# Alibi attention and a SwiGLU block on one core: loads in order of need, masks derived on chip, four tiles ahead of the FFN

## The chip, the core and the metric

One NeuronCore of a Trainium2 chip. The metric is the time of one execution on the device in microseconds (us), lower is better; the median of three runs of the kernel before is 411.18 us (411.11 to 411.30).

## What is computed

q, k and v have 8 batches, 8 heads, 576 positions and 64 columns. Attention looks back over 128 positions with a bias that falls with the distance; its output, 4608 rows of 512 columns, goes through a SwiGLU block of width 1536. Cut to what matters:

```python
scores = scale * np.matmul(q, k.transpose(0, 1, 3, 2))
slopes = 2.0 ** (-8.0 * (np.arange(H) + 1) / H)
mask = (rel >= 0) & (rel < 128)            # rel = query position - key position
scores = np.where(mask, scores - slopes[:, None, None] * np.abs(rel), -1e9)
attn = softmax(scores)
x = np.matmul(attn, v).transpose(0, 2, 1, 3).reshape(B * S, H * D)
g = x @ w_gate
out = (g * sigmoid(g) * (x @ w_val)) @ w_out
```

Inputs and output are float32; on the chip everything that TensorE reads is float16.

## The kernel before

**Tiles and units.** The eight batches are taken as four pairs (s = 0 to 3). A pair has nine tiles of 128 rows: four of the first batch, one made of the last 64 rows of both (two DMAs per tensor), and four of the second batch. Tiles are numbered 0 to 35 over the pairs (`ranks`). A pair also has nine units (queries of 128 rows); unit i needs the tiles up to `need_rank[i]`, which for a pair are 1, 2, 3, 4, 6, 7, 8, 8, 8.

**Attention for a unit** has four steps. The tile's k and q (`kn`, `qn`) are transposed on TensorE into one PSUM tile `pt` (L162, L164) and copied by VectorE to `kT` and `qT` (L165, L166). Scores `ps` (L209) go through ScalarE's exp into `exr` (L223) and are multiplied on VectorE with a mask that holds the bias and the window (L227). With those as weights TensorE takes v, whose 65th column is ones (`va`, L254); VectorE divides by that column (L256, L257) into `x`. TensorE transposes x (`px`, L281), and ScalarE copies it to `xT` (L282).

**Masks.** There are four, all loaded over the queue of SyncE: `reg` for most units, `lo` and `hi` for the units beside the shared tile, `com` for the shared tile itself.

**The FFN** runs over nine blocks of 512 rows. Block n takes units 4n and so on (block 0: units 0 to 3; block 8: the four shared units). For each of 12 slices m of 128 columns a generator `gate_val` does four matmuls for the gate (`pg`, L295), tanh on ScalarE (L298), a VectorE step `uu` (L300), four matmuls for the value (`pv`, L308) and their product `hT` (L310). A `pg` with its `pv` is called a pair here, each of the two a group. The projection of block n-1 (`po`, L322, 12 matmuls for each of four row tiles) is mixed into block n after m = 1 to 4.

**Order.** Code order is mixed by hand: `att_step` advances attention by one of eight steps per unit, and after each FFN step as many are taken as keep 4.55 units per 36 FFN steps. `ready[n]` says how many units must be finished ahead of block n. A scheduler then fixes each engine's order. Tile i + 8 is loaded in unit i, and the transposes for unit i + 2 are issued in unit i, two units ahead of need. In front of block 0 stand units 0 to 3, with the transposes up to tile 7 and the scores of unit 4.

**Loads.** k, q, v and the three weights are loaded over GpSimd's queue (POOL), which turns float32 into float16. In order: tiles 0 and 1; columns 0 to 128 of the gate and value weights; tiles 2 and 3; columns 128 to 512; tile 4; columns 512 to 1536 of both; tile 5; w_out; tiles 6 and 7; the rest as buffers come free (four of k and q, 14 of v). Each DMA waits, on POOL, for the landing of the eighth before it.

Of the kernel before, what the change touches and what calls it, by code (L numbers as in the profile page):

```python
# [10 lines left out]
FP16 = mybir.dt.float16  # L11
# [6 lines left out]
QK_BY_DMA = False  # L18
X_BY_DMA = False
# [7 lines left out]
def slot_c(h):  # L27
    return 4 * (h % 2) + h // 2


def make_masks(H):

    slopes = [2.0 ** (-8.0 * (h + 1) / H) for h in range(H)]
    j = np.arange(P)[:, None]
    i = np.arange(P)[None, :]

    def weight(h, u, ok):
        return np.where(ok & (u >= 0) & (u < WIN), np.exp(-slopes[h] * np.maximum(u, 0)), 0.0)

    reg = np.zeros((P, H, 256), np.float32)  # L40
    lo = np.zeros((P, H, 256), np.float32)
    hi = np.zeros((P, H, 256), np.float32)
    com = np.zeros((P, H, 128), np.float32)
    every = np.ones((P, P), bool)
    for h in range(H):
        s = slot(h)
        diag = weight(h, i - j, every)
        for m in (reg, lo, hi):
            m[:, s, 0:128] = diag
        reg[:, s, 128:256] = weight(h, i - j + 128, every)  # L50
        lo[:, s, 128:256] = weight(h, i - j + 128, (i < 64) & every)
        hi[:, s, 128:256] = weight(h, i - 64 - j + 128, (i >= 64) & every)
        com[:, slot_c(h), :] = weight(h, i - j, (i < 64) == (j < 64))
    return [m.astype(np.float16) for m in (reg, lo, hi, com)]
# [3 lines left out]
def kernel(  # L58
# [16 lines left out]
    NSUP = B // 2  # L75
    scale = 1.0 / np.sqrt(D)

    reg, lo, hi, com = make_masks(H)
# [5 lines left out]
    mask = {}  # L84
    for name, m in (("reg", reg), ("lo", lo), ("hi", hi), ("com", com)):
        m_d = nc.inline_tensor(m, name="mask_" + name)
        mask[name] = (consts.tile(list(m.shape), FP16, name="m_" + name), m_d)

    def load_mask(name):
        t, d = mask[name]  # L90
        nc.sync.dma_start(t, d.ap())

    load_mask("reg")
# [9 lines left out]
    vpool = ctx.enter_context(tc.tile_pool(name="vp", bufs=14))  # L103
# [4 lines left out]
    hpool = ctx.enter_context(tc.tile_pool(name="hp", bufs=2))  # L108
# [4 lines left out]

    units = []
    for s in range(NSUP):
        for p in range(9):
            units.append(dict(s=s, p=p))  # L120
    ranks = [(s, r) for s in range(NSUP) for r in range(9)]

# [6 lines left out]
    def pieces(s, c):  # L129
        if c == 4:  # L130
            return [(0, 64, 2 * s, 512), (64, 128, 2 * s + 1, 512)]
        b, t = (2 * s, c) if c < 4 else (2 * s + 1, c - 5)
        return [(0, 128, b, t * P)]

    def load(rank):
        s, c = ranks[rank]
        tq = nat.tile([P, H, D], FP16, name="qn", tag="qn")
        tk = nat.tile([P, H, D], FP16, name="kn", tag="kn")
        tv = vpool.tile([P, H, D + 1], FP16, name="va", tag="va")
        nc.gpsimd.memset(tv[:, :, D:D + 1], 1.0)  # L140
        for t_, src in ((tk, k), (tq, q), (tv, v)):
            for p0, p1, b, r0 in pieces(s, c):
                nc.gpsimd.dma_start(  # L143
                    t_[p0:p1, :, 0:D],
                    src[b, :, r0:r0 + p1 - p0, :].rearrange("h p d -> p h d"))
        natq[rank], natk[rank], va[(s, c)] = tq, tk, tv

    def transposes(rank):
        s, c = ranks[rank]
        if c == 0:  # L150
            qTs[s] = tpool.tile([P, 4, 9 * P], FP16, name="qT", tag="qT")
            kTs[s] = tpool.tile([P, 4, 9 * P], FP16, name="kT", tag="kT")
        cols = slice(c * P, (c + 1) * P)
        tq, tk = natq.pop(rank), natk.pop(rank)
        if QK_BY_DMA:
            for t_, dst in ((tk, kTs[s]), (tq, qTs[s])):
# [3 lines left out]
        pt = ps_a.tile([P, 8, P], FP16, name="pt", tag="a")  # L160
        for j in range(4):
            nc.tensor.transpose(pt[:, j, :], tk[:, 2 * j:2 * j + 2, :], idm)  # L162
        for j in range(4):
            nc.tensor.transpose(pt[:, 4 + j, :], tq[:, 2 * j:2 * j + 2, :], idm)  # L164
        nc.vector.tensor_copy(kTs[s][:, :, cols], pt[:, 0:4, :])  # L165
        nc.vector.tensor_copy(qTs[s][:, :, cols], pt[:, 4:8, :])  # L166
# [3 lines left out]
    def scores(i):  # L170

        s, p = units[i]["s"], units[i]["p"]
# [3 lines left out]
        if p == 8:  # L176
# [9 lines left out]

            def act(par):
                nc.scalar.activation(er[:, 4 * par:4 * par + 4, :], banks[par], AF.Exp, scale=scale)

            def mul():  # L190
                nc.vector.tensor_mul(e, er, mask["com"][0])

            return [[lambda: act(0)], [lambda: act(1), mul], [], []]
# [25 lines left out]
        m = mask["lo" if p == 3 else "hi" if p == 7 else "reg"][0]  # L219
# [14 lines left out]
    def weighted(i):  # L234

        s, p = units[i]["s"], units[i]["p"]
        x = xpool.tile([P, H, D], FP16, name="x", tag="x")
        xs[i] = x
        for half in range(2):
            av = ps_a.tile([P, 4, D + 1], FP32, name="av", tag="a")  # L240
            todo = []
            for j in range(4):
                h = 4 * half + j
                if p == 8:
                    todo.append((j, ex[(s, 3)][:, slot(h), 128:256], va[(s, 3)][:, h, :]))
                    todo.append((j, ex[(s, 7)][:, slot(h), 128:256], va[(s, 8)][:, h, :]))
# [15 lines left out]
    def place(i):  # L262

        s, p = units[i]["s"], units[i]["p"]
        if p == 8:
            return 8, s
# [212 lines left out]
```

## Time and profile before

| | |
|---|---|
| median of three runs | 411.18 us |
| the profiled execution | 410.85 us |
| its span, first to last instruction | 409.1 us |
| TensorE busy | 364.4 us, 89% |
| VectorE busy | 245.9 us, 60% |
| ScalarE busy | 173.8 us, 42% |
| mean granted TensorE clock | 0.997 |
| read from HBM, written | 39.62 MB, 9.44 MB |

TensorE's busy time counts pipelined matmuls and is no measure of how well its array is used; what matters is where it is idle, and who ended that. In the rows of the profile an instruction is named by its line in the kernel, its engine, and what it writes and reads, as `kT<-pt`; PE is TensorE, PEld its weight loads, DVE VectorE, ACT ScalarE, POOL GpSimd, SP SyncE.

### The profile page before, as it was taken

To read this page: it belongs to the slowest core of one execution; us is meant where nothing else is said; L and a number is where in the kernel's file an instruction comes from. 1 tells how busy PE (TensorE), PEld (TensorE's weight loads), DVE (VectorE), ACT (ScalarE), POOL (GpSimd) and SP (SyncE) were. 2 spreads that over 40 slices of the span, in tenths; PEclk is the share of its full clock that TensorE was granted. 3 is DMA by queue.
4 is the path that set the end of the run, shared out by engine and by line. 5 is a ranking of instruction groups with operands and counts; after the bars stand their busy time and mean duration, and the time that the engine had idled before them with its cause. 6 is when DMAs were issued, how large, how long until landed. Compare 5 with 4: busy or idle time off the path is not lost.

```text
span 409.1 us, 6645 instructions
## 1 busy us (share of the span) xinstructions
PE 364.4 (89%) x2592; PEld 181.0 (44%) x2592; DVE 245.9 (60%) x500; ACT 173.8 (42%) x317; POOL 112.0 (27%) x170
## 2 busy tenths in 40 slices
PE   0571289999999999999999999999999999999995
PEld 0240134455545445444454454455544445444442
DVE  0351057876587567675885586758865864572550
ACT  1241055534455455445644555455444543323321
POOL 7974485053424211542260104111000000000000
PEclk9999999999999999999999999999999999999998
DMA  9999999269969652799696527654011000101104
GB/s 221 164 192 193 182 155 95 14 42 80 124 66 66 64 79 38 52 82 116 64 68 63 79 38 48 82 79 29 0 53 51 2 27 26 51 2 51 54 12 91
DMA packets 124304, 30.62 MB, mean 75 GB/s; under 512 B 114544, under 2 KB 119152, under 8 KB 124272
## 3 DMA queue, kind: packets, MB, share of 16 engines
q0 software_dynamic: 118304, 18.88, 62.0%
q1 hardware_dynamic: 5968, 11.31, 8.1%
q8 instruction: 20, 0.33, 0.3%
q14 instruction: 12, 0.10, 0.1%
HBM read 39.62 MB, written 9.44 MB: 120 GB/s over the span
## 4 chain that ended last, share of the span: by engine, by line
PE 73%; DMA 10%; DVE 7%; ACT 5%; issue 2%; POOL 1%; DVEq 0%; POOLq 0%; ACTq 0%
PE po L322 22%; PE pv L308 20%; PE pg L295 20%; DMA kn<-in_k_dram 6%; DMA wv_sb<-in_moe_w_val_dram 4%; ACT exr L223 4%; PE ps L209 3%; PE av L254 3%; PE px L281 3%; DVE uu L300 2%; PE pt L162 1%; PE pt L164 1%; DVE hT L310 1%; DVE exl L227 1%; DVE ex L227 1%
## 5 line engine op out<-in xcount | busy, mean ns | idle before, releaser
L308 PE MATMUL pv<-xT,wv_sb 128*128 128x512 f16 x432 | 112.0, 380 | 1.4 <-DVE uu L300 1.2
L295 PE MATMUL pg<-xT,wg_sb 128*128 128x512 f16 x432 | 112.0, 381 | 0.3
L300 DVE SCALAR_TENSOR_TENSOR uu<-tt,pg 128x512 f16<-128x512 f16 x108 | 73.8, 684 | 61.6 <-ACT tt L298 61.2
L322 PE MATMUL po<-wo_sb,hT 128*128 128x512 f16 x432 | 104.8, 379 | 0.9 <-ACT osb L326 0.7
L298 ACT ACTIVATE tt<-pg 128x512 f16<-128x512 f32 x108 | 65.1, 603 | 79.5 <-PE pg L295 77.6
L223 ACT ACTIVATE exr<-ps 128x512 f16<-128x512 f32 x128 | 67.4, 608 | 39.7 <-PE ps L209 39.7
L310 DVE TENSOR_TENSOR hT<-uu,pv 128x512 f16<-128x512 f16 x108 | 74.0, 685 | 8.3 <-PE ps L209 1.0
L143 POOL DMA_DIRECT2D kn<-in_k_dram x40 | 34.0, 853 | 113.3 <-PE pt L164 101.9
L308 PEld LDWEIGHTS <-wv_sb 128*128 128x128 f16 x432 | 40.8, 98 | 47.4 <-issue 4.4
L322 PEld LDWEIGHTS <-hT 128*128 128x128 f16 x432 | 40.0, 98 | 43.7 <-issue 3.9
L295 PEld LDWEIGHTS <-wg_sb 128*128 128x128 f16 x432 | 39.9, 98 | 43.8 <-issue 3.2
L227 DVE TENSOR_TENSOR ex<-exr,m_reg 128x1024 f16<-128x1024 f16 x48 | 33.1, 689 | 36.2 <-ACT exr L223 36.2
L326 ACT ACTIVATE osb<-po 128x512 f32<-128x512 f32 x36 | 21.6, 600 | 59.0 <-PE po L322 58.9
L282 ACT COPY xT<-px 128x512 f16<-128x512 f16 x36 | 21.0, 584 | 50.9 <-PE px L281 50.8
L162 PE MATMUL pt<-idm,kn 128*128 128x128 f16 x144 | 15.7, 238 | 27.9 <-DMA kn<-in_k_dram 27.0
L143 POOL DMA_DIRECT2D va<-in_v_dram x40 | 33.8, 851 | 7.3 <-POOL va L140 5.0
L143 POOL DMA_DIRECT2D qn<-in_q_dram x40 | 34.1, 854 | 5.1 <-DMA wo_sb<-in_moe_w_out_dram 2.9
L165 DVE COPY kT<-pt 128x512 f16<-128x512 f16 x36 | 15.1, 418 | 31.6 <-PE pt L164 31.4
L257 DVE TENSOR_TENSOR x<-av,rec 128x256 f16<-128x256 f32 x72 | 29.0, 419 | 0.7
L209 PE MATMUL ps<-qT,kT 64*128 64x256 f16 (+1 forms) x288 | 27.2, 282 | 2.3 <-DVE qT L166 2.3
L162 PEld LDWEIGHTS <-kn 128*128 128x128 f16 x144 | 11.1, 105 | 35.4 <-DMA kn<-in_k_dram 29.1
L281 PE MATMUL px<-idm,x 128*128 128x128 f16 x144 | 18.8, 230 | 5.5 <-DVE x L257 5.4
(27 smaller groups left out, 173.5 us busy)
## 6 DMA issues: line engine op xcount, KB each, us to landing
out_dram<-osb SPq DMA_DIRECT2D x32, 256.0 KB, 2.0
kn<-in_k_dram POOLq DMA_DIRECT2D x32, 128.0 KB, 3.7
qn<-in_q_dram POOLq DMA_DIRECT2D x32, 128.0 KB, 5.0
va<-in_v_dram POOLq DMA_DIRECT2D x32, 128.0 KB, 5.3
wo_sb<-in_moe_w_out_dram POOLq DMA_DIRECT2D x2, 768.0 KB, 16.4
wg_sb<-in_moe_w_gate_dram POOLq DMA_DIRECT2D x2, 512.0 KB, 8.7
wv_sb<-in_moe_w_val_dram POOLq DMA_DIRECT2D x2, 512.0 KB, 10.1
out_dram<-osb SPq DMA_DIRECT2D x8, 128.0 KB, 2.3
```

Source lines behind the costliest of these rows:

```text
L143: nc.gpsimd.dma_start(t_[p0:p1, :, 0:D], src[b, :, r0:r0 + p1 - p0, :].rearrange("h p d -> p h d"))
L162: nc.tensor.transpose(pt[:, j, :], tk[:, 2 * j:2 * j + 2, :], idm)
L209: nc.tensor.matmul(two[par][:, j, o:o + w], kT[rows, pair, kcols], qT[rows, pair, cols], start=(j == 0 and n == 0), stop=(j == 1 and n == ...
L223: nc.scalar.activation(er[:, o:o + 2, :], banks[q4][par], AF.Exp, scale=scale)
L227: nc.vector.tensor_mul(e[:, o, :], er[:, o, :], m[:, o, :])
L281: nc.tensor.transpose(pt[:, kb, :], x[:, kb * P:(kb + 1) * P], idm)
L295: nc.tensor.matmul(pg, wg_sb[:, kb, ms], xT[n][:, kb, :], start=(kb == 0), stop=(kb == NKB - 1))
L298: nc.scalar.activation(tt, pg, AF.Tanh, scale=0.5)
L300: nc.vector.scalar_tensor_tensor(out=uu, in0=tt, scalar=1.0, in1=pg, op0=ALU.add, op1=ALU.mult)
L308: nc.tensor.matmul(pv, wv_sb[:, kb, ms], xT[n][:, kb, :], start=(kb == 0), stop=(kb == NKB - 1))
L310: nc.vector.tensor_mul(hT[n][:, m, :], uu, pv)
L322: nc.tensor.matmul(po, hT[n][:, m, j * P:(j + 1) * P], wo_sb[:, m, :], start=(m == 0), stop=(m == NMB - 1))
```

## The change

- **Loads** are ordered anew, and k, q and v of a tile are loaded separately: k and q of tile 0, then q, v and k so that each unit's last need comes last, up to tile 4's k (v of tile 4 later); then columns 0 to 128 and 128 to 512 of the two weights; tile 5 and v of tile 4; columns 512 to 1024; tile 6; columns 1024 to 1536; tiles 7 and 8; w_out.
- **Masks**: only `reg` is loaded. `lo`, `hi` and `com` are put together by memsets and copies on VectorE; `com` takes the heads in the same order as the others, for which the exps of the shared unit write with a stride.
- **v's column of ones** is set once for 14 fixed buffers by VectorE, not by POOL for each tile.
- **Transposes**: q and k have a PSUM tile each, q goes first (but for a pair's first tile), and they are issued with the scores that need them, one unit ahead, not two.
- **FFN**: the scores of unit 4 and the transposes for them follow unit 3's end in the code. The first eight FFN steps of block 0 have no attention between them, the other 16 have two attention steps each, and later blocks 5.2 units per 36 steps.
- **hT** has a buffer for each m (18 of them) instead of one for each block (two).

The core of the diff:

```diff
-    load_mask("reg")
+    def make_lo():
+
+        nc.vector.memset(lo[:, :, 192:256], 0.0)
+        nc.vector.tensor_copy(lo[:, :, 0:192], reg[:, :, 0:192])
+
+    def make_hi():
+
+        nc.vector.memset(hi[:, :, 128:192], 0.0)
+        nc.vector.tensor_copy(hi[:, :, 0:128], reg[:, :, 0:128])
+        nc.vector.tensor_copy(hi[:, :, 192:256], reg[:, :, 128:192])
+
+    def make_com():
+
+        nc.vector.memset(com, 0.0)
+        nc.vector.tensor_copy(com[0:64, :, 0:64], reg[0:64, :, 0:64])
+        nc.vector.tensor_copy(com[64:128, :, 64:128], reg[64:128, :, 64:128])
...
+    def transposed(name, rank):
+
+        s, c = divmod(rank, 9)
+        t_, dst = (natk.pop(rank), kTs[s]) if name == "k" else (natq.pop(rank), qTs[s])
+        pt = ps_a.tile([P, 4, P], FP16, name="pt", tag="a")
+        for j in range(4):
+            nc.tensor.transpose(pt[:, j, :], t_[:, 2 * j:2 * j + 2, :], idm)
+        nc.vector.tensor_copy(dst[:, :, c * P:(c + 1) * P], pt)
...
+        for name in ("kq" if c == 0 else "qk"):
+            transposed(name, rank)
...
-            if i < last:
+            if i < last and i != FIRST - 1:
                 transposes_to(need_rank[i + 1])
                 after = scores(i + 1)
-            for n in range(4):
-                for f in after[n]:
+            if i == 1:
+                make_lo()
+            if i == 5:
+                make_hi()
+                make_com()
+            for fs in after:
+                for f in fs:
                     f()
-                if n == 2 and i + 2 <= last:
-                    transposes_to(need_rank[i + 2])
                 yield i
             weighted(i)
             yield i
-            loads_to(i + 8)
+            if i >= FIRST:
+                loads_to(i + 7)
...
+            if i == FIRST - 1:
+
+                transposes_to(need_rank[i + 1])
+                for fs in scores(i + 1):
+                    for f in fs:
+                        f()
+                    yield i + 1
...
-    loads_to(1)
-    load_w(wg2, wg_sb, 0, 128)
-    load_w(wv2, wv_sb, 0, 128)
-    loads_to(3)
...
+    load_qk(0, "kq")
+    for r in range(4):
+        load_qk(r + 1, "q")
+        load_v(r)
+        load_qk(r + 1, "k")
+    load_w(0, 128)
+    load_w(128, 512)
+    load(5)
+    load_v(4)
+    load_w(512, 1024)
+    load(6)
+    load_w(1024, 1536)
+    load(7)
+    load(8)
+    loaded = 9
...
+    for _ in ffn():
         step += 1
-        target = base + step * (4.55 * 8) / per_block
-        while att_done < target and att_step():
-            att_done += 1
+        if step < 24:
+            blk, target = 0, base + 2 * max(0, step - 8)
+        else:
+            blk = min(NBLK - 1, 1 + (step - 24) // 36)
+            target = base + 32 + (step - 24) * RATE * 8 / 36
```

What this does to the engines' order, at three places. First POOL, which issues the loads. Before, from the third slice of the gate weight on (`kn_134` is tile 4, `kn_149` tile 5, `kn_158` tile 6):

```order
L143 DMA kn_134<-in_k_dram 64x8x64 x2
...
L344 DMA wg_sb_65<-in_moe_w_gate_dram 128x4x512
L344 DMA wv_sb_66<-in_moe_w_val_dram 128x4x512
...
L143 DMA kn_149<-in_k_dram 128x8x64
L143 DMA qn_148<-in_q_dram 128x8x64
L143 DMA va_150<-in_v_dram 128x8x64
L404 DMA wo_sb_67<-in_moe_w_out_dram 128x6x512 x2
L140 MEMSET va_159 128x8
L143 DMA kn_158<-in_k_dram 128x8x64
```

The two rows of 512 columns stand there twice. Now, on POOL from the first such slice's predecessor on (`kn_142` is tile 5, `kn_151` tile 6, `kn_158` now tile 7):

```order
L407 DMA wg_sb_65<-in_moe_w_gate_dram 128x4x384
L407 DMA wv_sb_66<-in_moe_w_val_dram 128x4x384
L149 DMA kn_142<-in_k_dram 128x8x64
L149 DMA qn_144<-in_q_dram 128x8x64
L143 DMA va2_102<-in_v_dram 128x8x64
...
L407 DMA wg_sb_65<-in_moe_w_gate_dram 128x4x512
L407 DMA wv_sb_66<-in_moe_w_val_dram 128x4x512
L149 DMA kn_151<-in_k_dram 128x8x64
L149 DMA qn_153<-in_q_dram 128x8x64
...
L149 DMA kn_158<-in_k_dram 128x8x64
```

Tile 5 has moved ahead of four slices of 512 columns, tile 6 ahead of two of them and of w_out, and w_out behind tile 8.

Second, VectorE ahead of the first FFN step `uu`. Before, after unit 3's masks `exl` (`pt_377` is tile 5, `pt_388` tile 6, `pt_457` tile 7, `ex_452` unit 4; the first `uu` comes seven rows below):

```order
L227 TENSOR_TENSOR exl_372<-exr_371,m_lo_61 128x1024 x2
L165 COPY kT_174<-pt_377 128x4x128
L166 COPY qT_173<-pt_377 128x4x128
L165 COPY kT_174<-pt_388 128x4x128
L166 COPY qT_173<-pt_388 128x4x128
...
L257 TENSOR_TENSOR x_401<-av_402,rec_411 128x256
...
L227 TENSOR_TENSOR ex_452<-exr_451,m_reg_60 128x1024
L165 COPY kT_174<-pt_457 128x4x128
```

Now, after unit 3's x (`pt_505` and `pt_511` are q and k of tile 5):

```order
L269 TENSOR_TENSOR x_400<-av_413,rec_422 128x256
L163 COPY qT_170<-pt_505 128x4x128
L163 COPY kT_171<-pt_511 128x4x128
L307 SCALAR_TENSOR_TENSOR uu_439<-tt_437,pg_432 128x512
L314 TENSOR_TENSOR hT_431<-uu_439,pv_441 128x512
```

Of tiles 5, 6 and 7 and unit 4's scores only tile 5 still stands ahead of the FFN.

Third, VectorE further on in block 0, from the fifth pair on (`uu_503`; `pt_517`, `pt_523` are tile 6, `pt_565`, `pt_571` tile 7, `pt_668` tile 8):

```order
L163 COPY qT_170<-pt_517 128x4x128
L307 SCALAR_TENSOR_TENSOR uu_503<-tt_501,pg_496 128x512
L163 COPY kT_171<-pt_523 128x4x128
L314 TENSOR_TENSOR hT_495<-uu_503,pv_546 128x512
L239 TENSOR_TENSOR ex_542<-exr_541,m_reg_60 128x1024 x2
L307 SCALAR_TENSOR_TENSOR uu_563<-tt_561,pg_556 128x512
L163 COPY qT_170<-pt_565 128x4x128
L163 COPY kT_171<-pt_571 128x4x128
L314 TENSOR_TENSOR hT_555<-uu_563,pv_594 128x512
```

The copies of tiles 6 and 7, which stood ahead of the FFN, are now within its fifth and sixth pair.

More of the change, by code (lines that the diff above doesn't have):

```diff
@@ L112 @@
     ps_a = ctx.enter_context(tc.tile_pool(name="ps_a", bufs=4, space=PSUM))
[L117 to L121, printed above, removed]
+    NV = 14
+    va_all = []
+    for n in range(NV // 2):
+        tv = consts.tile([P, 2, H, D + 1], FP16, name=f"va{n}")
+        nc.vector.memset(tv[:, :, :, D:D + 1], 1.0)
+        va_all += [tv[:, 0], tv[:, 1]]
+    units = [(s, p) for s in range(NSUP) for p in range(9)]
+    last = len(units) - 1
+    NR = 9 * NSUP
     def col_of(p):
@@ L159, in transposes @@
             return
[L160 to L166, printed above, removed]
+        for name in ("kq" if c == 0 else "qk"):
+            transposed(name, rank)
     ex = {}
     def scores(i):
-        s, p = units[i]["s"], units[i]["p"]
+        s, p = units[i]
         c = col_of(p)
@@ L329, in project @@
             yield
-    NBLK = NTOK // 512
     def ffn():
@@ L340, in ffn @@
             yield from project(NBLK - 1, j, ps_a, "a", 4)
[L343 to L350 removed]
+    need_rank = [9 * s + r for s in range(NSUP) for r in (1, 2, 3, 4, 6, 7, 8, 8, 8)]
     loaded = done_t = 0
```

217 lines of the change are left out of this document (86 added, 131 removed).

## The prediction

> **What bounds the kernel now.** I read the page's slices first, then busy time by stage, then the timeline of TensorE and of the queues, then the groups by line.
>
> The slices of 10.2 us each, TensorE's busy share and that of the DMA engines:
>
> ```profile
> PE   0571289999999999999999999999999999999995
> DMA  9999999269969652799696527654011000101104
> ```
>
> TensorE is idle for much of the first six slices, while the DMA engines are full; from then on it is the other way round. By stage (busy us of PE, PEld, DVE, ACT, POOL, granted clock, DMA share, GB/s):
>
> ```profile
> 0.00:59.30 59.30, 23.11 (x185) 13.07 (x185) 15.94 (x42) 14.25 (x27) 42.65 (x71) 1.00 1.76 185
> 59.30:91.30 32.00, 31.21 (x239) 15.69 (x239) 26.03 (x53) 15.81 (x30) 12.44 (x18) 1.00 0.87 57
> 91.30:320.00 228.70, 226.30 (x1722) 113.43 (x1722) 159.34 (x332) 115.42 (x214) 56.95 (x83) 1.00 0.64 64
> ```
>
> After 59.3 us TensorE is idle 0.8 us of 32.0 and 2.4 us of 228.7: nothing but less matmul work would shorten that part. Before it, 36.2 us of 59.3 are idle. TensorE's own rows say for what (start, duration, and in brackets the idle time before and who ended it):
>
> ```profile
> 9.35 0.61 PE L162 MATMUL pt<-idm,kn 128*128 128x128 f16 x4 [9.35 <-DMA kn<-in_k_dram]
> 38.89 0.61 PE L162 MATMUL pt<-idm,kn 128*128 128x128 f16 x4 [7.86 <-DMA kn<-in_k_dram]
> 49.03 0.61 PE L162 MATMUL pt<-idm,kn 128*128 128x128 f16 x4 [8.69 <-DMA kn<-in_k_dram]
> 59.29 1.89 PE L295 MATMUL pg<-xT,wg_sb 128*128 128x512 f16 x4
> 91.33 1.02 PE L295 MATMUL pg<-xT,wg_sb 128*128 128x512 f16 x4
> ```
>
> The three waits are for k of tiles 0, 5 and 6. Tiles 5 and 6 aren't needed by FFN block 0 (it takes units 0 to 3, so tiles 0 to 4), but their transposes stand ahead of units 2 and 3 on TensorE, and their loads stand behind eight weight slices and half of w_out on the one load queue. So block 0 starts at 59.29, and block 1 at 91.33.
>
> **The load queue.** Its first issues, the masks on the other queue, what one transfer is (KB, median us from issue to landing), and two stretches in which only w_out and only tiles move:
>
> ```profile
> 1.27 1.01 POOL L143 DMA_DIRECT2D kn<-in_k_dram  x1 [0.40 <-issue]
> 2.27 0.89 POOL L143 DMA_DIRECT2D qn<-in_q_dram  x1
> 2.08 0.43 SPq L91 DMA_DIRECT2D m_hi<-mask_hi  x1
> 2.56 0.43 SPq L91 DMA_DIRECT2D m_com<-mask_com  x1
> ...
> m_hi<-mask_hi SPq DMA_DIRECT2D x1, 512.0 KB, 6.8
> m_com<-mask_com SPq DMA_DIRECT2D x1, 256.0 KB, 7.2
> kn<-in_k_dram POOLq DMA_DIRECT2D x32, 128.0 KB, 3.7
> wo_sb<-in_moe_w_out_dram POOLq DMA_DIRECT2D x2, 768.0 KB, 16.4
> wg_sb<-in_moe_w_gate_dram POOLq DMA_DIRECT2D x2, 512.0 KB, 8.7
> wg_sb<-in_moe_w_gate_dram POOLq DMA_DIRECT2D x1, 384.0 KB, 6.8
> wg_sb<-in_moe_w_gate_dram POOLq DMA_DIRECT2D x1, 128.0 KB, 8.0
> ...
> 41.50:44.50 3.00, 0.00 (x0) 0.00 (x0) 0.00 (x0) 0.00 (x0) 1.11 (x3) 1.00 1.25 207
> 50.00:60.00 10.00, 8.14 (x66) 4.40 (x66) 4.74 (x15) 4.42 (x9) 9.65 (x19) 1.00 2.43 155
> ```
>
> A tile of k, q or v is 131 kB at 155 GB/s, 0.85 us. A 512-column slice is 524 kB at 207, 2.53; a 384 slice 1.90; half of w_out 3.80; a 128 slice lies between the two rates, 0.63 to 0.85, I take 0.75. Test: from tile 0's k (9.35) to tile 5's k (38.89) the queue holds 15 tiles and slices of 1.5 + 3.8 + 10.1, together 28.1; measured 29.54. I scale by 1.05. That it comes out says that the queue is served in order and never empty.
>
> The first k took 8 us to land, where the median is 3.7. In that time four masks, three of 512 KB and one of 256, 1.8 MB in all, were on the other queue. The change leaves one, 0.5 MB. I take 3.7 after an issue a little before 1.27, so a first landing at 5.0; the other end is 9.35, no gain here.
>
> New queue order, landings by these prices. Tile 4's k: 13 tiles on, 11.6 more, 16.6; POOL's 13 issues at 0.9 before it and 3.7 for its own landing put it nearer 17.0. Then slices 128 and 384 of both matrices (5.3) and k, q of tile 5 (1.7), times 1.05: **23.9**, against tile 5 at 38.89 before. Then v of 5 and 4, two 512 slices, k and q of tile 6: 8.5 x 1.05, **32.8**. Then v 6, two 512 slices, k and q of tile 7: 7.6 x 1.05, **40.8**. Tile 8 and w_out end at 52, before block 1 wants them.
>
> **When the FFN starts.** On the new TensorE order the transposes of tile 5 stand ahead of the last transposes of unit 3 and of block 0. The steps from there have rows; the chain's rows (start, duration) give the FFN's groups cold and warm:
>
> ```profile
> 58.03 0.40 PE L281 MATMUL px<-idm,x 128*128 128x128 f16 x2
> ...
> 59.36 1.82 PE pg L295 x4
> 61.18 1.27 PE pv L308 x4
> 62.45 0.22 PE pt L162 x4
> 62.90 0.86 PE pg L295 x4
> ```
>
> From the last pair of px to the first pg it was 1.26 us. Tile 5: two groups of transposes at 0.61, overlapping, 0.9; so 23.9 + 0.9 + 1.26 = **26.0**. The other path, unit 3 behind tile 4 at 17.0 (scores, four exps of 0.6, masks, weighting, px), needs some 7 us and is done by about 24.5. So the FFN starts 33.3 us earlier.
>
> **Block 0.** Its first eight groups have no attention between them: 8 x 0.86 and (1.82 + 1.27 - 1.72) = 1.4 for the cold ones, to 34.3. Then a gate (0.86), tile 6's transposes (0.44, landed at 32.8), a pv (0.86), unit 4's scores, a gate (0.86): 38.0 with scores as below. There stand tile 7's transposes, which land at 40.8: a new wait of 2.8 us. What follows is dense in VectorE work, since units 4 to 7 (two steps of attention for each FFN step, before about one) fall into eight pairs. Its prices:
>
> ```profile
> L310 DVE TENSOR_TENSOR hT<-uu,pv 128x512 f16<-128x512 f16 x108 | 74.0, 685 | 8.3 <-PE ps L209 1.0
> L300 DVE SCALAR_TENSOR_TENSOR uu<-tt,pg 128x512 f16<-128x512 f16 x108 | 73.8, 684 | 61.6 <-ACT tt L298 61.2
> L227 DVE TENSOR_TENSOR ex<-exr,m_reg 128x1024 f16<-128x1024 f16 x48 | 33.1, 689 | 36.2 <-ACT exr L223 36.2
> L257 DVE TENSOR_TENSOR x<-av,rec 128x256 f16<-128x256 f32 x72 | 29.0, 419 | 0.7
> L165 DVE COPY kT<-pt 128x512 f16<-128x512 f16 x36 | 15.1, 418 | 31.6 <-PE pt L164 31.4
> L256 DVE RECIPROCAL rec<-av 128x4 f32<-128x4 f32 x72 | 10.9, 169 | 4.8 <-PE av L254 4.8
> ...
> L209 PE MATMUL ps<-qT,kT 64*128 64x256 f16 (+1 forms) x241 | 19.0, 258 | 0.0
> L254 PE MATMUL av<-va,ex 128*128 128x65 f16 x312 | 15.9, 193 | 0.2
> ...
> 64.00:80.00 16.00, 15.61 (x117) 7.70 (x116) 13.40 (x27) 9.25 (x18) 5.75 (x8) 1.00 0.90 58
> ```
>
> From tile 7's copies to the end of unit 7 VectorE has 4 copies (1.7), one hT and six pairs (8.9), 7 mask products (4.8), 8 reciprocals and 8 x (4.7): 20.1 us. TensorE has in the same stretch two tiles (0.9), 13 groups (11.2), 24 score matmuls at 0.079 (1.9), 64 of av at 0.051 (3.3), 16 px (0.9): 18.2. So VectorE is the bound there. The 64 to 80 row has it at 84% with TensorE at 98%; where it is the bound I take 95%: 21.1 from 41.1, then the 1.26 to the next gate: block 1 starts at **63.4**, where before it was 91.33, a gain of 27.9. Block 0 is 37.4 long, 5.4 longer than before.
>
> **The rest.** From block 1 to the end it was 409.1 - 91.33 = 317.8. At that point the new order has 7 of block 0's w_out matmuls done, the old one 12, and it lacks two scores: 5 x 0.215 + 0.2, 1.3. RATE 5.2 against 4.55 only draws attention forward: per block VectorE has 12 pairs (16.4) and 5.2 units of 3.4, 34.1, TensorE 36 groups (31.0) and 5.2 units of 2.1, 41.9: 81%, below the 84% that left TensorE 98% busy. The scores now follow their tile's copies closely, and transposes take two PSUM buffers instead of one: between nothing and 0.3 us for each of 27 tiles, 8 us; nearest is this row of the waits after 62 us, where px follows x just as closely:
>
> ```profile
> PE px L281 <- DVE x L257: 0.7, 3, 0.4
> ```
>
> So I take 1.5 in all. Smaller hT tiles (18 of one m) cost nothing: block n+1's m = 6 takes the buffer of m = 0, which the last projection left two pairs earlier.
>
> The masks made on VectorE are 4,096 columns of copies; at the 689 ns per 1,024 above, 2.8 us at most. They run where VectorE has nothing yet:
>
> ```profile
> 11.18 0.42 DVE L165 COPY kT<-pt 128x512 f16<-128x512 f16 x1 [11.18 <-PE pt L164]
> ```
>
> Without that cover tile 1's copies would be late by up to 2.8, still ahead of tile 4 at 17.0. So nothing. The memsets that leave POOL and come to VectorE lie off the path as well.
>
> **Sum.** 63.4 + 317.8 + 1.3 + 1.5 = 384.0 of span. The profiled execution had 1.75 more than its span (410.85), and the median is 0.33 above that: **386**.
>
> **A rule against the change.** In the rows above POOL issues a tile's DMA in 0.9 us with VectorE idle or on PSUM. The Trainium skill, SBUF — State Buffer, Who interferes with whom, says that copies within SBUF in VectorE's two-port mode shut GpSimd out for the whole instruction, so that descriptors wait. No row here has such a copy. As a mechanism of this kernel: the mask copies, up to 2.8 us by the product's row, stop POOL in the first 12 us, where issue (0.9) is as slow as the transfer (0.85), so all later landings slip by as much: 388.8. On the wait for tile 7 the chain has 1.4 us as the price of a cold start after a long idle. By the Trainium skill, TensorE: Matmul & The Clock Gate, Part 1, about 3.4 us of idleness bring the cold clock back; 2.8 would stay below, and no run here shows that limit.
>
> **The rivals.**
> - *The first load is slow by itself* (a start-up of the software queue, not the masks). For it: no row shows a first load without the masks beside it. Against it: 1.3 MB of masks that go are 6 us at 207 GB/s, more than the 4.35. All landings 4.35 later: 390.4. Chance 0.15.
> - *VectorE keeps up* and tile 7 is early enough: TensorE alone bounds block 0, 38.0 + 18.2 + 1.26, block 1 at 57.5: 380. For it: the 98% in the 64 to 80 row. Against: 20.1 is more than 18.2. Chance 0.13.
> - *The copies stop POOL*: 388.8, chance 0.08.
> - *The scores wait for their copies.* The transposes had a lead of a unit and now stand two FFN matmuls (0.43 us) ahead of the scores that need the copy. VectorE, 81% busy, may take longer. At 0.3 us a tile it is 394, chance 0.07. Each tile that waits 0.93 us (25 us over 27) eats the whole gain; beyond that the kernel is slower than before, say 414 at 1.05. Against it: px with the same lead waited 0.7 us in all. Chance 0.03.
> - *The change doesn't do what it says*: the FFN still waits for late loads, as the queue isn't served in issue order. The test of 28.1 against 29.54 speaks against it. About 400 to 411, chance 0.02, half of it faster.
>
> **How the numbers follow.** The forecast has 0.52, with 383 to 389 as its own range (first landing 1 us either way, VectorE at 90 to 100%, the rest 0 to 3). The range from 379 to 395 takes in the first three rivals and the small wait; what is left out is under 2 in 10. A measurement of this kernel can tell about 0.2%, 0.8 us, from no change. Faster: 0.52 + 0.15 + 0.13 + 0.08 + 0.07 + 0.01 = 0.96; same 0.01; slower 0.03.
>
> **What would show it.** Right: first kn transposes near 5, first pg near 26, one TensorE wait of 2 to 4 us for kn or qn after the fifth pg, VectorE over 90% busy from there to block 1, block 1's first pg near 63, and the stages after it as long as before. Wrong: first k near 9; a gap on POOL beside VectorE's copies; waits of ps for qT after 70 us; a first pg later than 32.

## The result, and the profile after

| | before | after |
|---|---|---|
| median, same chip | 411.14 us (410.30 to 411.30) | 388.65 us (388.14 to 389.88) |
| ratio | | 0.9461 (95%: 0.9435 to 0.9487) |
| profiled execution, its span | 410.85, 409.1 us | 388.84, 387.1 us |

The forecast was 386 in a range of 379 to 395. The slices of the page, now 9.7 us each, TensorE and the DMA engines:

```profile
PE   1889899999999999999999999999999999999994
DMA  9999999999897369599441956310011001001013
```

The half-idle slices of TensorE are gone but the first. By stage, cut where block 0 and block 1 start (busy us of PE, PEld, DVE, ACT, POOL, then granted clock, DMA share, GB/s):

```profile
0.00:30.40 30.40, 18.37 (x152) 11.28 (x153) 17.23 (x51) 11.67 (x21) 25.33 (x35) 1.00 1.77 148
30.40:66.40 36.00, 33.42 (x262) 16.14 (x262) 27.73 (x58) 18.14 (x35) 23.40 (x29) 1.00 1.98 173
66.40:300.00 233.60, 232.09 (x1803) 116.75 (x1800) 163.81 (x348) 119.10 (x222) 59.94 (x72) 1.00 0.77 66
```

TensorE is now idle 12.0 us before block 0, 2.6 within it, and 1.5 of the next 233.6. The clock column reads 1.00 in the first stage too, although a group of four transposes takes 0.61 us there and 0.40 in block 0: where TensorE is slow has to be read from its rows. The rows at the steps of the forecast:

```profile
5.58 0.61 PE L162 MATMUL pt<-idm,kn 128*128 128x128 f16 x4 [5.58 <-DMA kn<-in_k_dram]
...
16.61 0.40 PE L291 MATMUL px<-idm,x 128*128 128x128 f16 x2 [0.88 <-DVE x L269]
...
21.56 0.40 PE L291 MATMUL px<-idm,x 128*128 128x128 f16 x2 [0.75 <-DVE x L269]
...
26.52 0.39 PE L291 MATMUL px<-idm,x 128*128 128x128 f16 x2 [0.75 <-DVE x L269]
...
30.48 1.87 PE L302 MATMUL pg<-xT,wg_sb 128*128 128x512 f16 x4 [0.67 <-ACT xT L292]
...
44.87 0.40 PE L162 MATMUL pt<-idm,qn 128*128 128x128 f16 x4 [1.58 <-DMA qn<-in_q_dram]
...
66.46 1.02 PE L302 MATMUL pg<-xT,wg_sb 128*128 128x512 f16 x4
```

First k at 5.58 (before 9.35); the units follow one another every 4.95 us; block 0 starts at 30.48 (59.29) and waits for one load, 1.58 us, q of tile 7; block 1 starts at 66.46 (91.33). From there to the end it is 387.1 - 66.46 = 320.6 us, before 317.8. The first gate was ended by `xT`, the last step of unit 3, not by a load. Yet the chain of work that ended last doesn't run through unit 3 (start, length, what):

```profile
22.00 10.49 DMA wg_sb<-in_moe_w_gate_dram
...
32.78 12.04 DMA qn<-in_q_dram
...
44.87 0.62 PE pt L162 x8
```

It comes from the load queue: q of tile 7, issued at 32.78, landed 12.04 us later. The FFN's start has 1.58 us of slack; what bounds the stretch up to 44.87 is the queue. The issue of q of tile 5, and its way to landing:

```profile
L149 POOL DMA_DIRECT2D qn<-in_q_dram x1: 903/903/903, 18.9 to 18.9; - x1
...
DMA to landing us min/median/max: 8.8/8.8/8.8
```

18.9 + 8.8: it landed at 27.7, forecast 23.9. Windows of the trace show the queue below its earlier speed there (GB/s is the last number):

```profile
16.00:20.00 4.00, 3.31 (x25) 1.98 (x26) 2.33 (x7) 1.71 (x4) 3.73 (x6) 1.00 1.49 136
20.00:24.00 4.00, 3.16 (x33) 2.17 (x31) 2.88 (x8) 1.60 (x4) 3.38 (x5) 1.00 1.31 163
```

Before, the same two windows had 163 and 192.

### The profile page after: what moved, and what is told of

It reads as the page before. It is cut to its first block, busy times and chain, and to the rows that moved or that the text cites. A ratio compares the mean times of both kernels' runs of the same rounds, so it can differ in the third digit from the quotient of the medians.

```text
span 387.1 us, 6587 instructions
## 1 busy us (share of the span) xinstructions
PE 365.6 (94%) x2592; PEld 181.1 (47%) x2592; DVE 250.2 (65%) x515; ACT 173.8 (45%) x317; POOL 108.7 (28%) x134
## 4 chain that ended last, share of the span: by engine, by line
PE 77%; DMA 6%; DVE 6%; POOL 5%; ACT 4%; issue 2%; DVEq 0%; POOLq 0%; ACTq 0%
PE po L326 22%; PE pv L312 21%; PE pg L302 21%; PE ps L221 4%; PE pt L162 3%; PE av L266 3%; DMA qn<-in_q_dram 3%; DMA wg_sb<-in_moe_w_gate_dram 3%; ACT exr L235 2%; PE px L291 2%; DVE hT L314 2%; POOL qn L149 1%; POOL kn L149 1%; POOL va L143 1%; DVE ex L239 1%
## 5 line engine op out<-in xcount | busy, mean ns | idle before, releaser
L312 PE MATMUL pv<-xT,wv_sb 128*128 128x512 f16 x432 | 116.4, 382 | 0.0
L302 PE MATMUL pg<-xT,wg_sb 128*128 128x512 f16 x432 | 114.0, 381 | 0.7 <-ACT xT L292 0.7
L221 PE MATMUL ps<-qT,kT 64*128 64x256 f16 (+1 forms) x288 | 28.8, 274 | 0.7 <-DVE kT L163 0.3
L291 PE MATMUL px<-idm,x 128*128 128x128 f16 x144 | 19.8, 230 | 4.1 <-DVE x L269 3.8
L266 PEld LDWEIGHTS <-ex 128*128 128x128 f16 x384 | 18.8, 101 | 8.3 <-issue 2.2
L163 DVE COPY qT<-pt 128x512 f16<-128x512 f16 x36 | 14.9, 421 | 12.0 <-PE pt L162 11.8
L221 PEld LDWEIGHTS <-kT 64*128 64x128 f16 x288 | 13.4, 96 | 19.4 <-issue 15.2
## 6 DMA issues: line engine op xcount, KB each, us to landing
wg_sb<-in_moe_w_gate_dram POOLq DMA_DIRECT2D x2, 512.0 KB, 10.3
```

The lines of the kernel that those rows point to most:

```text
L221: nc.tensor.matmul(two[par][:, j, o:o + w], kT[rows, pair, kcols], qT[rows, pair, cols], start=(j == 0 and n == 0), stop=(j == 1 and n == ...
L266: nc.tensor.matmul(av[:, j, :], w, val, start=(n == 0), stop=(n == len(todo) - 1))
L302: nc.tensor.matmul(pg, wg_sb[:, kb, ms], xT[n][:, kb, :], start=(kb == 0), stop=(kb == NKB - 1))
L312: nc.tensor.matmul(pv, wv_sb[:, kb, ms], xT[n][:, kb, :], start=(kb == 0), stop=(kb == NKB - 1))
```

## The experiments

**Which part makes the gain.** Three kernels undo one part each.

*Old load order.* The kernel after with the loads of before:

```diff
-    load_qk(0, "kq")
-    for r in range(4):
-        load_qk(r + 1, "q")
-        load_v(r)
-        load_qk(r + 1, "k")
+    load(0)
+    load(1)
     load_w(0, 128)
+    load(2)
+    load(3)
...
+    for a0 in (0, 6):
+        nc.gpsimd.dma_start(wo_sb[:, a0:a0 + 6, :], wo2[:, a0:a0 + 6, :])
+    load(6)
     load(7)
     load(8)
```

> The kernel after, with the load order of before (whole tiles, w_out ahead of tile 6). My theory: the new load order carries the gain, and the work order only as far as loads allow. At 0.85 us a tile and 2.53 a slice tile 5 lands near 36, tile 6 near 48, tile 7 near 51; the FFN can still start after unit 3 (near 31) and its first eight groups and a gate are done by 39, so it waits once, some 8 us, for tile 6 and then, for 2 us or so, for tile 7. Block 1 starts 6 to 8 us later than after: 395 to 397. Rival A, the order of work alone makes the gain and loads do not matter: 388 to 390. Rival B, the load order is everything: near before, 405 or more.

Measured 394.23 us, ratio 0.9600 (0.9575 to 0.9625). TensorE's rows, and a window behind the wait:

```profile
32.48 1.87 PE L302 MATMUL pg<-xT,wg_sb 128*128 128x512 f16 x4 [0.67 <-ACT xT L292]
...
47.57 0.61 PE L162 MATMUL pt<-idm,qn 128*128 128x128 f16 x4 [3.34 <-DMA qn<-in_q_dram]
...
72.12 1.02 PE L302 MATMUL pg<-xT,wg_sb 128*128 128x512 f16 x4
```

```profile
47.50:49.00 1.50, 1.43 (x10) 1.14 (x11) 0.78 (x2) 0.00 (x0) 1.50 (x3) 0.50 2.47 154
```

The wait for tile 6 came where expected but was 3.34 long, not 8: TensorE had more groups to do first than I counted. Tile 7 made none. In its place came a cost not expected: after 3.34 us of idleness the granted clock was 0.50. Both rivals fall, and the time is a little below the expected 395 to 397; undoing the loads costs 5.6 us. Block 1 starts 5.7 us later than in after: 2.0 by the FFN's later start, 1.8 by the longer wait, and 1.9 that are left, of which the slow clock is a part.

*Old lead.* The new loads, but tiles 6 and 7 and the scores of unit 4 ahead of the FFN:

```diff
-            if i < last and i != FIRST - 1:
+            if i < last:
...
+                if n == 2 and i + 2 <= last:
+                    transposes_to(need_rank[i + 2])
                 yield i
...
-            if i == FIRST - 1:
...
```

> The kernel after with its new loads, but with tiles 6 and 7 transposed ahead of the FFN as before (transposes two units ahead of need, scores of unit 4 ahead of block 0). My theory: tile 6 (36.8 us in after) and perhaps tile 7 (44.8) now stand ahead of block 0, so the FFN starts near 40 instead of 30.5 with fewer steps of attention left beside it; TensorE idles 8 to 10 us more, of which the attention already done gives some back: 394 to 400. Rival A, the load order alone makes the gain: 388 to 390. Rival B, the scores' closeness to their transposes costs time in the later blocks, so the longer lead gives some back: below 388.

Measured 400.34 us, 0.9736 (0.9709 to 0.9764).

```profile
37.19 0.61 PE L162 MATMUL pt<-idm,qn 128*128 128x128 f16 x4 [6.94 <-DMA qn<-in_q_dram]
...
45.04 0.61 PE L162 MATMUL pt<-idm,qn 128*128 128x128 f16 x4 [3.33 <-DMA qn<-in_q_dram]
...
49.67 1.89 PE L302 MATMUL pg<-xT,wg_sb 128*128 128x512 f16 x4
```

TensorE waits for tile 6 and then for tile 7 as well, so the FFN starts at 49.67, not 40: the mechanism was right, its size too small. Undoing the lead costs 11.7 us. Of the 22.5 us in all, then, load order and work order each hold a part that the other can't make: a load can't be waited for less if the work in front of the FFN still asks for it. The two parts are 17.3 us together; the other 5.2 were not taken apart. No run undoes both at once, and none undoes the separate PSUM tiles, the buffers of `hT` or the fixed column of ones.

*Masks loaded.* All four masks over SyncE's queue, no copies on VectorE:

```diff
-    nc.sync.dma_start(reg, reg_d.ap())
+    for t, m, name in zip((reg, lo, hi, com), make_mask(H), ("reg", "lo", "hi", "com")):
+        nc.sync.dma_start(t, nc.inline_tensor(m, name="mask_" + name).ap())
...
-            if i == 1:
-                make_lo()
```

> The kernel after with all four masks loaded at the start, as before, and no mask copies on VectorE. My theory: the 1.3 MB of masks delay the first k as in before, from 5.5 to about 9.3 us, and all landings with it; tile 7 lands at 48.6 instead of 44.8 and block 1 starts as much later: 391 to 393. Rival A, the start of the load queue is slow by itself and masks do not matter to it: first k at 5.5 still, 388.7. Rival B, the copies on VectorE hold up GpSimd's issues: without them landings come 1 to 3 us earlier, 386 to 388.

Measured 389.82 us, 0.9488 (0.9463 to 0.9513); the interval overlaps that of after.

```profile
9.28 0.61 PE L152 MATMUL pt<-idm,kn 128*128 128x128 f16 x4 [9.28 <-DMA kn<-in_k_dram]
...
32.90 1.86 PE L292 MATMUL pg<-xT,wg_sb 128*128 128x512 f16 x4 [0.67 <-ACT xT L282]
...
67.27 1.02 PE L292 MATMUL pg<-xT,wg_sb 128*128 128x512 f16 x4
```

```profile
L139 POOL DMA_DIRECT2D qn<-in_q_dram x1: 893/893/893, 21.4 to 21.4; - x1
...
DMA to landing us min/median/max: 6.5/6.5/6.5
...
L139 POOL DMA_DIRECT2D kn<-in_k_dram x1: 677/677/677, 15.8 to 15.8; - x1
...
DMA to landing us min/median/max: 5.5/5.5/5.5
```

The first k is back at 9.28, so the masks do hold up the first load; the rival of a slow start by itself is refuted. But q of tile 5 lands at 21.4 + 6.5 = 27.9, where after has 27.7: the 3.7 us of head start are gone by then, and tile 7 isn't waited for at all. My step "all later landings shift with the first" is refuted with it, and the 391 to 393 that rested on it. What the masks on chip are worth in time, about 1 us, can't be told from nothing.

Most of the head start goes in one place. The second issue shown is the last half of tile 4's k: it landed at 15.8 + 5.5 = 21.3, and from there to tile 5's q the queue took 6.6 us. In after, with the same order, it took 9.2 (18.5 to 27.7). With the masks loaded the slow stretch of the queue isn't there. The copies that this kernel lacks are over at 11.3 us in after, ahead of that stretch; why it is gone stays open.

**What bounds block 0.** *Tile 7 early*, ahead of the last columns of the two weights:

```diff
     load(6)
-    load_w(1024, 1536)
     load(7)
+    load_w(1024, 1536)
     load(8)
```

> The kernel after with tile 7 loaded ahead of columns 1024 to 1536 of the two weights. My theory: the one wait in block 0, 1.58 us for tile 7, goes; the columns land 2.5 us later and are wanted only by the ninth pair. TensorE, 96% busy behind that wait, keeps what it gains: 387.0, at most 1.6 better. Rival A, VectorE bounds the rest of block 0, as I forecast: what is gained is lost to it again, 388.4 to 388.9. Rival B, the weights now come late: a new wait for them in pair 9, 389 or more.

Measured 386.44 us, 0.9408 (0.9386 to 0.9431).

```profile
30.48 1.87 PE L302 MATMUL pg<-xT,wg_sb 128*128 128x512 f16 x4 [0.67 <-ACT xT L292]
...
64.33 1.02 PE L302 MATMUL pg<-xT,wg_sb 128*128 128x512 f16 x4
```

```profile
30.40:64.30 33.90, 32.94 (x262) 16.15 (x262) 27.49 (x58) 18.16 (x35) 21.88 (x26) 1.00 1.85 177
```

The FFN starts at the same 30.48, the wait is gone, and block 1 starts 2.1 us earlier: 1.58 for the wait, and 0.5 that I had not forecast. The gain stays, so rival A falls, and so does rival B. TensorE is busy 97% of block 0, VectorE 81%. That VectorE isn't the bound doesn't follow from the gain alone: in the forecast's sum its stretch begins with tile 7's copies, and would have moved forward with them. The busy times behind the wait tell it, below.

*The old rate* in the later blocks, `RATE = 4.55` instead of 5.2:

> The kernel after with 4.55 units of attention per 36 FFN steps in the later blocks instead of 5.2, nothing else; its first 66 us are the same program. My theory: TensorE bounds the later blocks in either case, so 388.2 to 389.2, the stretch behind block 1's start 320 to 321.5. Rival A, the higher rate crowds VectorE and costs (the 0 to 8 us that I allowed for): 1 us or more faster than after. Rival B, attention too late at 4.55 makes a block wait for its units: slower than 390. As the first 66 us are unchanged, its trace also tells whether the slow stretch of the load queue (16 to 30 us, 125 to 165 GB/s where before had 155 to 207) comes back: with the same program it should if the program causes it, and tile 5's q should land near 27.7 again; if it is chance, nearer 24 to 25.

Measured 388.05 us, 0.9446 (0.9431 to 0.9460).

```profile
65.83 1.02 PE L302 MATMUL pg<-xT,wg_sb 128*128 128x512 f16 x4
```

385.7 of span less 65.83 are 319.9, against 320.6: no difference that can be told, and neither rival's time. q of tile 5 was late again:

```profile
28.37 0.61 PE L162 MATMUL pt<-idm,qn 128*128 128x128 f16 x4 [0.42 <-DMA qn<-in_q_dram]
```

So the slow stretch of the queue belongs to the program, not to one execution. The wait for tile 7 was 0.47 us here, not 1.58, and block 1 started 0.6 earlier: two executions of the same first 66 us differ by as much, and the 0.5 left over with tile 7 early is no more than that.

**What sets the FFN's start.** *Units interleaved by hand*, with tile 7 early:

```diff
-        pt = ps_a.tile([P, 4, P], FP16, name="pt", tag="a")
+        pool, tag = (ps_f, "gv") if rank <= FIRST else (ps_a, "a")
+        pt = pool.tile([P, 4, P], FP16, name="pt", tag=tag)
...
+        transposes_to(3)
+        weighted(0)
+        all_of(2)
+        make_lo()
+        transposes_to(4)
+        weighted(1)
+        x_transposed(0)
+        all_of(3)
+        weighted(2)
+        x_transposed(1)
+        weighted(3)
+        x_transposed(2)
+        x_transposed(3)
```

> The kernel after with tile 7 ahead of columns 1024 to 1536, and units 0 to 3 interleaved by hand (transposes of the next tile and scores of the next unit ahead of a unit's av and px; transposes and px in the three PSUM banks that the FFN does not use yet). My theory: the chain of units, 4.95 us each, shortens to some 3.5 and ends near 26, but tile 5's transposes still stand ahead of the first gate and its q lands at 27.7 to 28.5, so the FFN starts at 29.5 to 30.5 and little is gained over the same kernel without it (386.4): 385.3 to 386.5. Rival, the chain of units alone sets the FFN's start: first gate near 26, 382 to 383.

Measured 385.85 us, 0.9394 (0.9367 to 0.9421), not to be told from 386.44.

```profile
27.92 0.50 PE L163 MATMUL pt<-idm,qn 128*128 128x128 f16 x3 [2.15 <-DMA qn<-in_q_dram]
...
29.31 1.78 PE L304 MATMUL pg<-xT,wg_sb 128*128 128x512 f16 x4
```

From 25.8 TensorE has nothing to do but half of unit 3's `px`, which stands behind tile 5, and waits 2.15 us for that; the FFN gains 1.2. So the rival, the chain alone, falls. Two things held the start at nearly the same time: the chain of units, and tile 5.

*Both taken away.* Besides, columns 512 to 1024 ahead of tile 5, whose transposes then stand behind the fifth gate:

```diff
     load_w(128, 512)
-    load(5)
-    load_v(4)
     load_w(512, 1024)
-    load(6)
-    load_w(1024, 1536)
+    load_qk(5)
+    load_qk(6)
+    load_v(4)
+    load_v(5)
     load(7)
+    load_w(1024, 1536)
+    load_v(6)
     load(8)
```

> The kernel after with the interleaved units and, besides, columns 512 to 1024 loaded ahead of tile 5, k and q of tiles 5 and 6 ahead of the v of 4 and 5, and tile 7 ahead of columns 1024 to 1536, so that tile 5's transposes stand behind the fifth gate. My theory, chain and loads together set the start: tile 4's k at 18.5 and 6.5 to 7.5 us of one unit put the first gate at 25 to 26, block 0 takes its 34 and 1 to 3 us of waits for tiles 5 and 6, block 1 starts at 60 to 63: 381 to 384. Rival A, the units keep their 4.95 us whatever their order (an engine, not the order, limits them): first gate at 30, 386 or more. Rival B, the loads bound all of block 0 and the earlier start turns into waits one for one: 386 to 387.

Measured 390.09 us, 0.9488 (0.9460 to 0.9516).

```profile
26.66 1.87 PE L304 MATMUL pg<-xT,wg_sb 128*128 128x512 f16 x4 [0.67 <-ACT xT L294]
...
51.50 0.38 PE L328 MATMUL po<-wo_sb,hT 128*128 128x512 f16 x1 [3.73 <-DMA wo_sb<-in_moe_w_out_dram]
...
67.52 1.02 PE L304 MATMUL pg<-xT,wg_sb 128*128 128x512 f16 x4
```

```profile
53.00:55.00 2.00, 2.00 (x20) 0.97 (x17) 0.97 (x3) 2.00 (x5) 0.00 (x0) 0.50 1.92 173
```

The start came at 26.66, 0.7 behind the expected 25 to 26 and far from rival A's 30: the theory of the start holds. The time didn't follow, for a reason none of the expectations had. The scheduler put one `po` matmul of block 0's projection between block 0's value and gate groups; on TensorE all else stood behind it until the first half of w_out landed: 3.73 us, and soon after it the granted clock was 0.50. Block 0 took 40.9 us, 7.0 more than with tile 7 early (33.9); the wait is 3.73 of them, and what the slow clock has of the rest wasn't told apart.

*Loads in the order that the start needs:* k and v of tile 4, which only unit 8 reads, behind tile 8; k and q of tile 5 ahead of columns 128 to 512; with the interleaved units:

```diff
     load_w(0, 128)
+    load_qk(5)
     load_w(128, 512)
-    load(5)
-    load_v(4)
     load_w(512, 1024)
-    load(6)
+    load_qk(6)
+    load_v(5)
+    load_qk(7)
+    load_v(6)
+    load_v(7)
     load_w(1024, 1536)
-    load(7)
     load(8)
+    load_qk(4, "k")
+    load_v(4)
```

> The interleaved units together with loads in the order of what the FFN's start needs: k and v of tile 4 behind tile 8, k and q of tile 5 ahead of columns 128 to 512, columns 512 to 1024 next, then k and q of 6 and 7, columns 1024 to 1536, tile 8, w_out. My theory: unit 3 is ready as before at 25 to 26 (26.66 with the interleaving so far) and tile 5 lands by 22 to 24, so neither holds the FFN: first gate at 25.5 to 26.7; block 0 takes its 33.5 to 34.5; block 1 at 59.5 to 61: 381.5 to 383.5. Rival A, the loads of weights now bound block 0 and the FFN waits for columns 128 to 512 or 512 to 1024: 384 to 386. Rival B, w_out or the columns from 1024 come too late for the earlier block, as w_out did with an early FFN before (3.7 us): 385 or more.

Measured 382.72 us, 0.9322 (0.9295 to 0.9350): faster than both kernels.

```profile
26.00 1.02 PE L306 MATMUL pg<-xT,wg_sb 128*128 128x512 f16 x4 [0.67 <-ACT xT L296]
...
60.55 1.02 PE L306 MATMUL pg<-xT,wg_sb 128*128 128x512 f16 x4
```

First gate at 26.00, block 0 of 34.55 us, the rest 380.7 - 60.55 = 320.2: within what was expected or at its edge. Of the 1.4 us by which block 0 is shorter than in after, two parts can be named: the wait for q of tile 7 is 0.75 instead of 1.58, and the first gate with its value group took 1.73 instead of 3.29. The second is TensorE at full speed from the first gate on.

**The queue between 14 and 30 us.** *k and v of tile 4 late* (its k is then transposed with unit 8's scores), nothing else:

```diff
-        load_qk(r + 1, "k")
+        if r < 3:
+            load_qk(r + 1, "k")
...
     load(5)
-    load_v(4)
...
     load(8)
+    load_qk(4, "k")
+    load_v(4)
```

> The kernel after with k and v of tile 4 (the shared tile, four DMAs of 64 partitions, wanted by unit 8 alone) moved behind tile 8 in the load queue, q of tile 4 left where it is; k of tile 4 is transposed with unit 8's scores. By bytes alone the queue gains 0.85 us for tile 5 and 1.7 for tile 7. Theory H, the half-tile DMAs cause the slow stretches of the queue behind them (16 to 24 and 26 to 30 us): both get faster beyond the bytes, q of tile 5 lands at 24.5 to 26, q of tile 7 at 41 to 42, and w_out and the rest follow. Theory O, something else slows the queue there: q of tile 5 at 26.5 to 28, of tile 7 at 42.8 to 43.5. The time by either: the wait for tile 7 (1.58) goes, the chain of units still sets the FFN's start near 30: 386.5 to 387.3; the landings, not the time, tell the theories apart.

Measured 386.80 us, 0.9422 (0.9397 to 0.9446). Issue and landing of q of tile 5:

```profile
L149 POOL DMA_DIRECT2D qn<-in_q_dram x1: 977/977/977, 17.4 to 17.4; - x1
...
DMA to landing us min/median/max: 7.8/7.8/7.8
```

And of tile 7:

```profile
L149 POOL DMA_DIRECT2D qn<-in_q_dram x1: 873/873/873, 30.2 to 30.2; - x1
...
DMA to landing us min/median/max: 11.5/11.5/11.5
```

They land at 25.2 and 41.7, that is 2.5 and 3.1 us earlier, where the bytes that left account for 0.85 and 1.7. This is theory H's forecast, and the time is within the 386.5 to 387.3 of both. Near the half tiles, which land at 46.6 to 47.4 now, the queue is slow again: 67 GB/s from 44 to 46 us, in after 170.

It doesn't show half tiles as the cause, though. Bytes aren't all that left: POOL issues each half in 0.7 us, and without the two of k the first slice of 384 columns is issued 1.1 us earlier (15.07, after 16.20). With the masks loaded the half tiles stand in the queue as in after, and the stretch behind them took 6.6 us, not 9.2. With the old load order that slice also took 3.6 us instead of 1.9 with no half tile ahead of it (v of tile 3 landed at 17.2, the slice at 20.8). And before's own half tiles, at 24 to 28 us, passed at 181 GB/s.

**The copies and GpSimd.** The first mask copy made eight times:

```diff
-        nc.vector.tensor_copy(lo[:, :, 0:192], reg[:, :, 0:192])
+        for _ in range(8):
+            nc.vector.tensor_copy(lo[:, :, 0:192], reg[:, :, 0:192])
```

> The kernel after with the first mask copy on VectorE (128 x 1536, 0.55 us) made eight times over, 3.9 us more of it at about 6.5 to 11 us; the output is unchanged. My theory, such copies hold up POOL's issues only a little (1.00 to 1.02 us beside one instead of 0.90): five or six issues of 1.0 to 1.1, landings 0.5 us later at most; VectorE itself is late by up to 3.9 us for unit 0, the chain of units starts up to 2 to 3 us later and the FFN with it, of which 1.6 is slack: 388.5 to 390.5. Rival, the copies stop GpSimd for their whole length: POOL issues of 1.4 to 1.5 us beside them, all landings 3 to 4 us later, tile 7 at 48: 391 to 393.

Measured 389.61 us, 0.9480 (0.9465 to 0.9496). POOL's issues beside the copies, and the first gate:

```profile
8.55 1.04 POOL L150 DMA_DIRECT2D qn<-in_q_dram  x1
9.58 1.18 POOL L144 DMA_DIRECT2D va<-in_v_dram  x1
```

```profile
31.89 1.86 PE L303 MATMUL pg<-xT,wg_sb 128*128 128x512 f16 x4 [0.67 <-ACT xT L293]
```

An issue takes 1.04 to 1.18 instead of 0.90, a little more than I expected and far from the rival's 1.4 to 1.5. Tile 7's q lands 1.0 us later (45.8), twice what I expected. The FFN starts 1.4 us later, since VectorE itself is late for unit 0; the time is 1.0 above that of after, with intervals that overlap.

## Why the prediction was right, and where it was not

**The sign and the mechanism.** Right: block 0 waited for tiles that it doesn't need, and the two kernels that undo the load order and the lead each lose by such waits. The size, 388.65 for 386, is in part luck. The forecast put block 1 at 63.4, it came at 66.46; the 3.1 us are the whole miss. They are 4.0 us by which tile 7's q was late (44.8, forecast 40.8), less 1.0 by which the stretch behind it was shorter (21.6, forecast 22.6). Of the signs that I named, the first k near 5 came and the stages after block 0 were as long as forecast. The first gate came at 30.48 and not near 26, the wait was 1.58 and not 2 to 4, VectorE was 86% busy behind it and not over 90, and block 1 came at 66.46 and not near 63.

**First load, 5.0.** 5.58; the masks are shown to be the cause of before's 9.35. **Landings, 17.0, 23.9, 32.8, 40.8.** Tile 4's k landed at 18.5, tile 5's q at 27.7, tile 6's at 36.7, tile 7's at 44.8. The sum has a slip: 23.9 is 16.6 plus 7.3, from the 17.0 that I had just chosen it would be 24.4, and all behind it 0.4 later. The step that failed is the price list: measured on stretches of before, it took the queue's speed as a property of the kind of transfer. 1.5 us were lost by tile 4's k, 0.6 of them at the first load, and 2.3 more by tile 5's q, where the slices and tiles ran below their prices. They stayed to the end; behind tile 5 the prices hold, 9.0 us to tile 6's q (8.9) and 8.1 on to tile 7's (8.0). The cause of the slow stretch stays open.

**FFN start, 26.0.** The step "the other path is done by about 24.5" failed. I gave unit 3 some 7 us behind tile 4, as if unit 2 were out of the way; on TensorE each unit's transposes stand behind the `px` of the unit two before, so units 0 to 2 come every 4.95 us: 16.61, 21.56, 26.52, and the gate at 30.48, 3.96 us behind. With the masks loaded, with k and v of tile 4 late and with eight copies the gate comes the same 3.96 us behind unit 2's `px` (28.94, 25.84, 27.93); only where tile 5's q came later still (old rate: 25.80, gate at 30.29) is it more. The loads set where the chain begins: it starts with tile 1's k, transposed at 10.20, which the forecast's prices put at 8.6. So some 1.6 of the 4.5 us are loads that came late, and the rest is the chain. With that chain shortened and the loads reordered the start was 26.00. Alone, the shorter chain moved it by 1.2; and with tile 5 at 25.2 but the chain as it was (k and v of tile 4 late) the first gate still came at 29.80.

**Wait for tile 7, 2.8.** 1.58; start and landing were both some 4 late, so it came out near by luck. **VectorE as the bound behind it.** Wrong in kind. From tile 7's transposes to block 1, in after:

```profile
44.87:66.46 21.59, 20.67 (x202) 10.75 (x203) 18.61 (x44) 12.48 (x24) 15.14 (x19) 1.00 2.11 167
```

TensorE is busy 96% of it and VectorE 86%, and of TensorE's 0.9 us of idleness one wait of 0.28 was ended by VectorE. I had left 7 `po` (7 x 0.215 = 1.5) and a part of the transposes out of TensorE's 18.2, and summed VectorE's durations, which overlap: its rows are 0.69 long and 0.61 apart. The rival "VectorE keeps up" was right on this point, though its 380 also took the 26.0 start.

**The rest, 1.5 for transposes, scores and the rate.** The stretch from block 1 on was met to a tenth (320.6), which is luck. The 1.3 for work left over is right: 5 more `po` and 2 more scores stand there. The 1.5 was for waits, but TensorE's idle time there fell from 7.7 to 6.9 us, while its busy time grew by 3.7; what the other busy time is wasn't found. With the old rate the stretch took 319.9. Waits of TensorE behind VectorE after 70 us:

```profile
PEld L221 <- DVE qT L163: 2.1, 5, 0.4
...
PE px L291 <- DVE x L269: 1.1, 4, 0.4
```

Five loads of weights for the scores wait 2.1 us in all, none over 0.4, and they overlap matmuls. The rival "the scores wait for their copies" is refuted.

**The rivals on the queue.** "The first load is slow by itself" falls by the loaded masks. "The copies stop POOL": the Trainium skill, SBUF — State Buffer, Who interferes with whom, speaks of a block for the whole instruction; here eight copies of 0.55 us made single issues longer by 0.14 to 0.28, so the direction agrees and the size is small. That this rival's 388.8 lies nearest to the measured 388.65 is chance.

**The clock.** After the 1.58 us wait a group of transposes took 0.40, at full clock. After 3.34 (old loads) it took 0.61, with 0.50 granted. The Trainium skill, TensorE: Matmul & The Clock Gate, Part 1, gives about 3.4 us of idleness. The wait of 1.58 stays well below it and 3.34 is just short of it, but the wait of 2.15 us in the last section doesn't fit it. What I called a cold start after a long idle had no long idle right before it: in before, TensorE was busy 8.4 of the 10.3 us ahead of the gate at 59.29. The price itself was right, and after pays it too: its first gate and value group took 3.29 us, two warm groups 1.72.

## What to carry to other kernels

In a lead-in, write down for the first real work both what it needs from the queue and the chain of dependent steps on each engine; here they ended close together, and taking away one moved the start to the other. Before naming an engine as the bound of a stretch, count every instruction of the others in it, projection and transposes included, and compare what each is busy in that stretch. Here a transfer put last, w_out, cost a wait as soon as one matmul that uses it was moved forward in TensorE's order.

## What the runs showed that was not expected

- One matmul that the scheduler moved forward cost 3.73 us of waiting, and afterwards the granted clock was 0.50 in a two-microsecond window.
- The clock can fall behind a shorter wait. Two matmuls of `px` took 0.27 us at 24.08, ahead of the 2.15 us wait for tile 5, and 0.42 at 28.22, behind it; the wait ends a thin stretch, and the FFN began like this (interleaved units):

```profile
24.00:29.30 5.30, 2.56 (x29) 1.76 (x27) 2.46 (x9) 1.28 (x3) 2.70 (x4) 0.83 2.06 163
29.30:31.00 1.70, 1.69 (x5) 0.64 (x5) 0.34 (x1) 0.00 (x0) 1.54 (x2) 0.54 1.24 207
```

  In after, without such a wait, the first gate was as slow, 1.87 us. With loads in order of need it took 1.02; there TensorE was busy 8.8 of the 10 us up to 26.0, in after 7.6 of the 10 up to 30.5. That this makes the difference isn't shown.
- Taking 0.26 MB of half-tile loads out of the queue moved the loads behind them by up to 1.7 us more than their bytes. A part is POOL's time to issue them; the rest is open.
